# Attention and squared-ReLU MLP on one core: one copy moved, one pair of sums moved, and the last store split in two

## The chip, the cores and the metric

The kernel runs on one core of one Trainium2 chip. The metric is the device time of one execution in microseconds (us). Before the change the median of three runs is 303.92 us (303.79 to 304.94). The profiled execution took 303.61 us; its trace spans 301.6 us from the first to the last instruction, and TensorE was granted 0.998 of its full clock.

## The reference

Attention over 8 batch rows of 8 heads, 576 positions and 64 dimensions. Heads 0 to 3 look at the last 32 positions ("sliding"), heads 4 to 7 at every fourth of the last 128 ("dilated"). The result, as a matrix of 4608 tokens by 512, goes through a two-layer perceptron whose hidden layer is a ReLU squared.

```python
scores = scale * np.matmul(q, k.transpose(0, 1, 3, 2))
mask_plain = (rel >= 0) & (rel < 32)
mask_dil = (rel >= 0) & (rel < 128) & (rel % 4 == 0)
scores = np.where(masks[None], scores, -1e9)          # plain for heads 0-3, dil for 4-7
attn = softmax(scores)
x = matmul(attn, v).transpose(0, 2, 1, 3).reshape(4608, 512)
h = x @ w_in                                           # 512 -> 2048
g = np.maximum(h, 0.0) ** 2
out = g @ w_out                                        # 2048 -> 512, float32
```

## The kernel before

**Two kinds of blocks.** Attention works by batch row (576 tokens, b = 0 to 7), the perceptron by chunk (512 tokens, c = 0 to 8). The attention result x is kept transposed, in f16, in a ring `xT` of 4 rows (2304 token columns, 4 groups of 128 features). Row 7's columns start at 7 x 576 modulo 2304 = 1728; chunk 7 reads columns 1280 to 1791 and chunk 8 columns 1792 to 2303.

**The order is written out by hand.** The perceptron of a chunk is a Python generator (`moe_gen`). `pump(n)` emits its next n steps, and the attention code calls `pump` between its own pieces, so that TensorE (PE) always finds matmuls between attention's waits. Each engine then runs its own queue strictly in the order of emission, and waits at an instruction whose semaphores are not there yet.

**First layer, `mm1_gen`, lines 318 to 333.** For each of 16 hidden blocks (`ffc`), four matmuls `ph <- xT, wi` (line 302) of 512 tokens, in two steps of two. Then ScalarE (ACT) writes `rt = relu(ph)` (line 327) and VectorE (DVE) squares it into `g` (line 328). So the first layer is 32 steps. There are four PSUM buffers for `ph` and its like (`pmool`), and two for the attention results (`papool`).

**Second layer, `mm2_strassen_gen`, lines 359 to 446, for chunks 2 to 8.** It takes seven products of half-sized blocks in place of eight, in the order A, C, A, half of B, A, the other half of B, A, B. Products with sums of blocks need sums of g: `sum_of_g` (lines 335 to 338) makes `gs[0]` and `gs[1]` on DVE from four hidden blocks at a time, once after block 11 and once after block 15. Three of the weight combinations stand ready in `wt`. Every product is 16 matmuls (`pa`, `pb` or `pc`, line 381) of 256 columns, and a whole one is four steps: one for every four matmuls, the last of which also emits what closes the product. Closing is a copy by ACT from PSUM into the output tile (`take`, line 397), or an addition by DVE (`add`, line 408). The output tiles are `ou` (upper 256 tokens) and `ov` (lower 256 tokens), and `leave` (line 403) stores them from the queue of SyncE (SP). In the last chunk they leave in four stores of 256 KB, each of 256 tokens by 256 columns.

**Attention values, rows 4 to 7, `attn_values_by_dma`, lines 759 to 782.** `av_sliding` computes weighted values (`pav`, line 642) for a third of the row, and `normalize` (lines 622 to 630) divides by the row sums on DVE: a reciprocal (line 625) and a multiplication (line 630) into `xs` or `xd`. The dilated half of x is transposed by DMA into `yd`, in two pieces, and `x_from` (line 695) copies each piece into its place in `xT` on ACT. The copy of a row's second piece is put into the list `second_half` and is emitted later. For row 7 that is after `pump(20)`, that is, behind hidden block 9 of chunk 7 (lines 933 to 937). Row 7's second piece fills columns 2048 to 2303.

**Attention values, rows 1 to 3, `attn_values`, lines 728 to 757.** Here `x_sliding` (lines 667 to 680) transposes `xs` by PE (`px`, line 671) as soon as two of its three parts are there. Row 3's attention values run beside the end of chunk 2's first layer and the beginning of its second.

Of the kernel before, what the change touches and what calls it, by code (L numbers as in the profile page):

```python
# [13 lines left out]
P = 128  # L14
# [3 lines left out]
def kernel(  # L18
# [9 lines left out]
    nc = tc.nc  # L28
# [11 lines left out]
    TOKC = 512  # L40
# [40 lines left out]
    HM = DM // 2  # L81
    HF = NFF // 2
    HTOK = TOKC // 2
# [181 lines left out]
    for m, w, pad in (  # L265
# [5 lines left out]
            out=lo_[:, 0:w], in0=relf[:, 0:w], scalar1=-pad - 0.5, scalar2=None, op0=ALU.is_gt  # L271
        )
        nc.vector.tensor_scalar(
            out=hi_[:, 0:w], in0=relf[:, 0:w], scalar1=W - pad - 0.5, scalar2=None, op0=ALU.is_lt
# [6 lines left out]
    for r in range(2):  # L281
        nc.vector.tensor_scalar(
            out=vd[r][:, 0, :, :, D],
# [12 lines left out]
    def mm1_half(c, ffc, ph, dmks, parts=None):  # L296
        lo = c * TOKC % XW
        cut = min(TOKC, XW - lo)
        parts = parts or [(0, cut, lo)] + ([(cut, TOKC, 0)] if cut < TOKC else [])
        for dmk in dmks:  # L300
            for t0, t1, x0 in parts:
                nc.tensor.matmul(  # L302
                    ph[:, t0:t1],
                    wi4[ffc // 4][:, dmk, :, ffc % 4],
                    xT[:, dmk, x0 : x0 + t1 - t0],
                    start=(dmk == 0 and t0 == 0),
                    stop=(dmk == NDM - 1),
                    skip_group_check=parts != [(0, TOKC, lo)],
                )
# [3 lines left out]
    def mm1_begin(c, ffc, parts=None):  # L313
        ph = pmool.tile([P, TOKC], FP32, name=f"ph{c}_{ffc}", tag="pm")
        mm1_half(c, ffc, ph, (0, 1), parts)
        return ph

    def mm1_gen(c, g, sums=False, begun=()):
        for ffc in range(NFF):
            if ffc < len(begun):  # L320
                ph = begun[ffc]
            else:
                ph = mm1_begin(c, ffc)
                yield
            mm1_half(c, ffc, ph, (2, 3), [(T0, TOKC, T0)] if begun and ffc < len(begun) else None)
            rt = osb.tile([P, TOKC], FP16, name=f"rt{c}_{ffc}", tag="rt")
            nc.scalar.activation(rt, ph[:], ACTF.Relu)  # L327
            nc.vector.tensor_mul(g[:, ffc, :], rt, rt)  # L328
            if c == 1 and ffc % 2 == 0:
                next(w_sums)  # L330
            if sums and ffc % 4 == 3 and ffc >= HF:
                sum_of_g(g, ffc - 3, ffc + 1)
            yield

    def sum_of_g(g, f0, f1):
        k = slice(f0 - HF, f1 - HF)
        nc.vector.tensor_add(gs[0][:, k], g[:, k, HTOK:], g[:, f0:f1, HTOK:])
        nc.vector.tensor_sub(gs[1][:, k], gs[0][:, k], g[:, k, 0:HTOK])
# [20 lines left out]
    def mm2_strassen_gen(c, g):  # L359
        A, Bk, Ck = "abc"  # L360
        banks = {}

        def wq(r, q):
            return lambda k: wo[2 * r + k // 4][:, k % 4, HM * q : HM * (q + 1)]

        def gq(i, r):
            return lambda k, t: g[:, HF * r + k, HTOK * i + P * t : HTOK * i + P * (t + 1)]

        def tq(n):
            return lambda k: wt[n][:, k]  # L370

        def sq(n):
            return lambda k, t: gs[n][:, k, P * t : P * (t + 1)]

        def product(bank, a, b, ts=(0, 1)):
            new = bank not in banks
            if new:
                banks[bank] = pmool.tile([P, 2, HM], FP32, name=f"p{bank}{c}", tag="pm")
            for t in ts:
                for k in range(HF):  # L380
                    nc.tensor.matmul(  # L381
                        banks[bank][:, t],
                        a(k, t),
                        b(k),
                        start=(new and t == 0 and k == 0),
                        stop=(k == HF - 1),
                        skip_group_check=True,
                    )
                    if k % 4 == 3 and (t, k) != (ts[-1], HF - 1):
                        yield  # L390

        def half(i):
            return otp.tile([P, 2, DM], FP32, name=f"o{i}_{c}", tag="ot")

        def take(o, j):
            ot = o[:, :, HM * j : HM * (j + 1)]
            nc.scalar.copy(ot, banks[A])  # L397
            return ot

        def leave(o, i, js):  # L400
            t0 = c * TOKC + HTOK * i
            m = slice(HM * js[0], HM * (js[-1] + 1))
            nc.sync.dma_start(
                out=out[t0 : t0 + HTOK, m].rearrange("(t p) m -> p t m", p=P), in_=o[:, :, m]
            )

        def add(ot, bank):
            nc.vector.tensor_add(ot, banks[bank], ot)  # L408

        last = c == NTOKC - 1  # L410

        nc.vector.tensor_sub(g[:, 0:HF, HTOK:], g[:, 0:HF, 0:HTOK], g[:, 0:HF, HTOK:])
        yield from product(A, gq(0, 0), wq(0, 0))
        upper = half("u")
        o11 = take(upper, 0)
        yield
        yield from product(Ck, gq(0, 1), wq(1, 0))
        add(o11, Ck)
        if last:
            leave(upper, 0, (0,))  # L420
        yield
        yield from product(A, sq(1), tq(1))
        lower = half("v")
        o21 = take(lower, 0)
        nc.vector.tensor_sub(gs[1], g[:, HF:, 0:HTOK], gs[1])
        yield
        yield from product(Bk, gq(1, 0), tq(2), (0,))
        yield
        yield from product(A, sq(0), tq(0))
        o22 = take(lower, 1)  # L430
        yield
        yield from product(Bk, gq(1, 0), tq(2), (1,))
        add(o22, Bk)
        if last:
            leave(lower, 1, (1,))
        yield
        yield from product(A, sq(1), wq(1, 1))
        take(upper, 1)
        leave(upper, 0, (1,) if last else (0, 1))
        while at_end:  # L440
            at_end.pop()()
        yield
        yield from product(Bk, gq(1, 1), tq(3))
        add(o21, Bk)
        leave(lower, 1, (0,) if last else (0, 1))
        yield

    def mm2(c, g, po, t, ffc):
# [57 lines left out]
    def moe_gen(c):  # L506
        g = hidden(c)
        yield from mm1_gen(c, g, c > 1)
        yield from (mm2_strassen_gen if c > 1 else mm2_gen)(c, g)
# [10 lines left out]
    def pump(n):  # L520
        for _ in range(n):
            while pending:
                try:
                    next(pending[0])
                    break
                except StopIteration:
                    pending.pop(0)
# [317 lines left out]

    g0 = hidden(0)
    pending.append(mm1_gen(0, g0, False, begun))
    pump(1000)
    pending.append(mm2_by_rows_gen(0, g0))
# [81 lines left out]
        attn_values_by_dma(b, (copied, load_and_turn, cast, load_rest))  # L931
        pump(1000)
    pending.append(moe_gen(B - 1))
    pump(20)
    second_half.pop()()
    pending.append(moe_gen(B))
    pump(10000)
# [30 lines left out]
```

## Time and profile before

| what | before |
| --- | --- |
| time, median of 3 | 303.92 us |
| span of the trace | 301.6 us |
| PE busy | 285.4 us (95%) |
| DVE busy | 212.9 us (71%) |
| ACT busy | 172.6 us (57%) |
| POOL (GpSimd) busy | 68.1 us (23%) |
| matmuls `ph`, line 302 | 648 in 134.6 us |
| ReLU `rt`, line 327 | 144 of 609 ns |
| square `g`, line 328 | 144 of 450 ns |
| copy `xT<-yd` of a second piece, line 695 | 4 of 1098 ns |
| sums of g, lines 337 and 338 | 14 of 693 ns and 14 of 692 ns |
| last addition `ov<-pb`, line 408, and its store | 692 ns; 256 KB, 2.2 us from issue to landing |

PE is busy nearly everywhere, so the rows with much busy time are not where this change works. What counts is the few places in which PE stands idle, and the time after its last matmul. They are found in the chain of work that ended last, and in the timeline of one engine at a time.

### The profile page before, as it was taken

The page shows a single profiled execution, that of the slowest core. Times are in us where ns is not written, and L with a number is a line of the kernel's source. Part 1 is how long each engine was busy: PE and PEld are TensorE (multiplying, and loading weights), DVE is VectorE, ACT ScalarE, POOL GpSimd, SP SyncE. Part 2 cuts the span into 40 slices and gives each one's busy share as a digit, 9 for nine tenths or more (in the row PEclk, how much of TensorE's full clock was granted, in tenths as well). Part 3 has the DMA queues.
Part 4 walks back from the last instruction along what each step waited for, and adds up shares of the span by engine and source line. Part 5 has one row for each costly group of instructions (what it writes and reads, how often), then busy time and mean ns, then how long its engine had stood idle before and what let it go on. Part 6 is the DMA issues. An engine that isn't in the chain of part 4 may idle for free.

```text
span 301.6 us, 6903 instructions
## 1 busy us (share of the span) xinstructions
PE 285.4 (95%) x2768; PEld 192.6 (64%) x2768; DVE 212.9 (71%) x439; ACT 172.6 (57%) x293; POOL 68.1 (23%) x112
## 2 busy tenths in 40 slices
PE   1889999999999999999999999999999998999994
PEld 1455554555554569656989986568656964785583
DVE  7784549668843999499849985998599733824651
ACT  1956648669745952585448554845585447326620
POOL 4491009002702700530125023502140000000000
PEclk9999999999999999999999999999999999999999
DMA  7899996999599989998999799999962230003013
GB/s 117 186 203 215 205 187 111 217 192 230 136 193 181 245 153 179 224 263 125 195 175 267 152 148 171 235 236 171 171 192 42 41 139 0 3 14 127 0 36 104
DMA packets 77375, 46.60 MB, mean 155 GB/s; under 512 B 58400, under 2 KB 69152, under 8 KB 77344
## 3 DMA queue, kind: packets, MB, share of 16 engines
q1 hardware_dynamic: 68592, 32.54, 51.5%
q0 software_dynamic: 8752, 13.63, 26.3%
q8 instruction: 21, 0.34, 0.5%
q14 instruction: 10, 0.08, 0.1%
HBM read 36.70 MB, written 16.52 MB: 176 GB/s over the span
## 4 chain that ended last, share of the span: by engine, by line
PE 87%; DVE 5%; DMA 3%; ACT 2%; issue 1%; POOL 0%; POOLq 0%
PE ph L302 40%; PE pa L381 16%; PE pb L381 8%; PE po L449 7%; PE pc L381 4%; DVE AT L574 3%; PE paw L658 3%; DMA nd<-in_q_dram 3%; PE pav L642 2%; PE pz L612 2%; PE ps L587 2%; ACT AT L571 1%; PE pf L515 1%; PE py L689 1%; DVE g L328 1%
## 5 line engine op out<-in xcount | busy, mean ns | idle before, releaser
L302 PE MATMUL ph<-xT,wi 128*128 128x512 f16 (+2 forms) x648 | 134.6, 356 | 1.1 <-ACT xT L695 1.0
L327 ACT ACTIVATE rt<-ph 128x512 f16<-128x512 f32 x144 | 85.7, 609 | 45.5 <-PE ph L302 43.8
L302 PEld LDWEIGHTS <-wi 128*128 128x128 f16 x648 | 68.8, 114 | 46.0 <-issue 1.3
L328 DVE TENSOR_TENSOR g<-rt 128x512 f16<-128x512 f16 x144 | 63.0, 450 | 36.5 <-ACT rt L327 35.2
L381 PEld LDWEIGHTS <-g 128*128 128x128 f16 x448 | 43.2, 98 | 6.3 <-DVE g L328 0.2
L381 PEld LDWEIGHTS <-gs 128*128 128x128 f16 x336 | 32.5, 98 | 3.7
L449 PE MATMUL po<-wo,g 128*128 128x512 f16 x128 | 33.1, 379 | 0.0
L169 POOL CAST vp<-sv 128x512 f16<-128x512 f32 x24 | 15.5, 677 | 56.2 <-DMA sv<-in_v_dram 44.3
L381 PE MATMUL pb<-wt,g 128*128 128x256 f16 x224 | 27.9, 273 | 0.0
L408 DVE TENSOR_TENSOR ov<-pb,ov 128x512 f32<-128x512 f32 x14 | 9.7, 692 | 25.2 <-PE pb L381 19.8
L381 PE MATMUL pa<-wt,gs 128*128 128x256 f16 x224 | 27.1, 272 | 0.0
L177 POOL CAST vd<-sd 128x512 f16<-128x512 f32 (+1 forms) x32 | 22.6, 731 | 13.6 <-DMA sd<-in_v_dram 11.5
L397 ACT COPY ov<-pa 128x512 f32<-128x512 f32 x14 | 8.2, 585 | 26.8 <-PE pa L381 26.8
L630 DVE TENSOR_TENSOR xd<-paw,rcp_d 80x512 f16<-80x512 f32 (+1 forms) x32 | 21.9, 685 | 1.1
L571 ACT ACTIVATE AT<-pz 128x576 f16<-128x576 f32 x32 | 19.8, 693 | 1.2 <-PE pz L612 1.1
L574 DVE TENSOR_TENSOR AT<-AT,maskd 128x576 f16<-128x576 f16 x32 | 19.4, 634 | 1.4 <-ACT AT L571 0.9
L574 DVE TENSOR_TENSOR AT<-AT,maskp 128x576 f16<-128x576 f16 x32 | 16.9, 547 | 4.6 <-ACT AT L571 3.5
L571 ACT ACTIVATE AT<-ps 128x576 f16<-128x576 f32 x32 | 19.2, 657 | 1.4 <-PE ps L587 0.8
L397 ACT COPY ou<-pa 128x512 f32<-128x512 f32 x14 | 8.2, 585 | 19.2 <-PE pa L381 19.2
L630 DVE TENSOR_TENSOR xs<-pav,rcp_p 96x512 f16<-96x512 f32 x24 | 16.5, 687 | 0.8
L449 PEld LDWEIGHTS <-g 128*128 128x128 f16 x128 | 10.4, 98 | 8.3
L658 PEld LDWEIGHTS <-AT 128*128 128x128 f16 x256 | 12.0, 98 | 5.4 <-PE px L671 1.0
(81 smaller groups left out, 276.6 us busy)
## 6 DMA issues: line engine op xcount, KB each, us to landing
sv<-in_v_dram SPq DMA_DIRECT2D x14, 288.0 KB, 5.3
dp<-nr SPq DMA_DIRECT2D x12, 288.0 KB, 4.1
out_dram<-ou SPq DMA_DIRECT2D x6, 512.0 KB, 4.9
out_dram<-ov SPq DMA_DIRECT2D x6, 512.0 KB, 5.6
sd<-in_v_dram SPq DMA_DIRECT2D x8, 320.0 KB, 5.0
ns<-in_k_dram POOLq DMA_DIRECT2D x8, 288.0 KB, 6.6
ns<-in_q_dram POOLq DMA_DIRECT2D x8, 288.0 KB, 8.3
sd<-in_v_dram SPq DMA_DIRECT2D x8, 256.0 KB, 5.7
```

What stands on the lines that cost most here:

```text
L169: nc.gpsimd.tensor_copy(vp[b % 2][:, m : m + 2, :, 0:D], sv[:, :, m : m + 2, :].rearrange("p h m d -> p m h d"))
L177: nc.gpsimd.tensor_copy(vd[b % 2][p0:P, t, c : c + 2, :, 0:D], sd[p0:P, t, :, D * c : D * (c + 2)].rearrange("p h (c d) -> p c h d", d=D),)
L302: nc.tensor.matmul(ph[:, t0:t1], wi4[ffc // 4][:, dmk, :, ffc % 4], xT[:, dmk, x0 : x0 + t1 - t0], start=(dmk == 0 and t0 == 0), stop=(dmk ...
L327: nc.scalar.activation(rt, ph[:], ACTF.Relu)
L328: nc.vector.tensor_mul(g[:, ffc, :], rt, rt)
L381: nc.tensor.matmul(banks[bank][:, t], a(k, t), b(k), start=(new and t == 0 and k == 0), stop=(k == HF - 1), skip_group_check=True,)
L397: nc.scalar.copy(ot, banks[A])
L449: nc.tensor.matmul(po, g[:, ffc, t * P : (t + 1) * P], wo[ffc // 4][:, ffc % 4, :], start=(ffc == 0), stop=(ffc == NFF - 1),)
L571: nc.scalar.activation(AT[:, u, 0:UW], ps[:, :, 0 : UW // 2], ACTF.Exp, scale=scale)
L574: nc.vector.tensor_mul(AT[:, u, 0:UW], AT[:, u, 0:UW], mask)
L630: nc.vector.tensor_tensor(out=x, in0=pv, in1=rb, op=ALU.mult)
L658: nc.tensor.matmul(pav[:, e, h * (D + 2) : h * (D + 2) + D + 1], AT[:, 4 + h, off : off + P], vd[b % 2][:, t, 2 * a + e, h, 0 : D + 1], st ...
```

## The change

Three edits, independent of each other.

1. Row 7's second piece of x is copied into `xT` after step 44 of chunk 7 in place of step 20. 44 steps are the 32 of the first layer and the first three products (4 steps each) of the second. The copy is meant to stand on ACT where no ReLU waits behind it.
2. In chunk 2 alone, the first two sums of g are emitted after the square of hidden block 12 in place of block 11. On DVE they so come behind the normalization of row 3's first third, not ahead of it.
3. In the last chunk, the last addition and its store are split into two halves of 128 tokens. The first half is stored from SP's queue, the second from ACT's. They are meant to overlap the first half's transfer with the second half's addition.

```diff
@@ mm1_gen @@
-            if sums and ffc % 4 == 3 and ffc >= HF:
-                sum_of_g(g, ffc - 3, ffc + 1)
+            if sums and ffc == (12 if c == 2 else 11):
+                sum_of_g(g, 8, 12)
+            if sums and ffc == 15:
+                sum_of_g(g, 12, 16)
@@ mm2_strassen_gen @@
         yield from product(Bk, gq(1, 1), tq(3))
-        add(o21, Bk)
-        leave(lower, 1, (0,) if last else (0, 1))
+        if last:
+            for t, eng in enumerate((nc.sync, nc.scalar)):
+                o = o21[:, t]
+                nc.vector.tensor_add(o, banks[Bk][:, t], o)
+                t0 = c * TOKC + HTOK + P * t
+                eng.dma_start(out=out[t0 : t0 + P, 0:HM], in_=o)
+        else:
+            add(o21, Bk)
+            leave(lower, 1, (0, 1))
         yield
@@ the end @@
     pending.append(moe_gen(B - 1))
-    pump(20)
+    pump(44)
     second_half.pop()()
     pending.append(moe_gen(B))
     pump(10000)
```

## The prediction

> **What bounds the kernel now.** I read the chain of work that ended last first, because PE is busy 95% of the span and only the chain tells which idle time moves the end. Its shares are on the page:
>
> ```profile
> PE 87%; DVE 5%; DMA 3%; ACT 2%; issue 1%; POOL 0%; POOLq 0%
> ```
>
> PE's matmuls carry 87% of it, so a change pays only where the chain leaves PE. Next I read the chain in order of time. Columns: start in us, length in us, engine, tile, line. It shows this around chunk 7:
>
> ```profile
> 244.14 8.65 PE ph L302 x40
> 252.79 0.02 issue
> 252.81 0.03 ACT rt L327
> 252.84 0.47 issue
> 253.31 1.06 ACT xT L695
> 254.37 0.04 issue
> 254.41 4.69 PE ph L302 x21
> ...
> 271.33 13.81 PE ph L302 x64
> ```
>
> Chunk 8's 64 matmuls run without a break in 13.81 us. Chunk 7's are cut by an ACT copy into `xT`. PE's own timeline (the bracket is idle time and what ended it) gives the true gap:
>
> ```profile
> 249.81 3.62 PE L302 MATMUL ph<-xT,wi 128*128 128x512 f16 x16
> 254.41 1.89 PE L302 MATMUL ph<-xT,wi 128*128 128x512 f16 x8 [0.99 <-ACT xT L695]
> ```
>
> The chain's 1.62 us hole (252.79 to 254.41) is not all idle: PE ran three more matmuls in it. It stopped 0.99 us before the fourth matmul of block 10.
>
> The other idle spot is in chunk 2. PE's and then DVE's timeline:
>
> ```profile
> 109.37 0.42 PE L642 MATMUL pav<-vp,AT 128*128 128x65 f16 x8 [0.60 <-DVE xs L630]
> ```
>
> ```profile
> 106.19 0.75 DVE L328 TENSOR_TENSOR g<-rt 128x512 f16<-128x512 f16 x2
> 106.98 0.69 DVE L337 TENSOR_TENSOR gs<-g 128x1024 f16<-128x1024 f16 x1
> 107.70 0.69 DVE L338 TENSOR_TENSOR gs<-gs,g 128x1024 f16<-128x1024 f16 x1
> 108.31 0.20 DVE L625 RECIPROCAL rcp_p<-pav 96x8 f32<-96x8 f32 x1
> 108.54 0.69 DVE L630 TENSOR_TENSOR xs<-pav,rcp_p 96x512 f16<-96x512 f32 x1
> 109.15 0.75 DVE L328 TENSOR_TENSOR g<-rt 128x512 f16<-128x512 f16 x2
> 109.81 0.20 DVE L625 RECIPROCAL rcp_p<-pav 96x8 f32<-96x8 f32 x1
> 110.05 0.69 DVE L630 TENSOR_TENSOR xs<-pav,rcp_p 96x512 f16<-96x512 f32 x1
> ```
>
> The third `pav` needs the PSUM buffer that the first normalization (108.54) frees, and that stands behind two sums. DVE has no idle time in these rows.
>
> Last, the end. PE stops at 297.39; this is SP's queue:
>
> ```profile
> 298.13 0.37 SPq L403 DMA_DIRECT2D out_dram<-ov  x1
> ```
>
> With 2.2 us from issue to landing, as the page's list of DMA issues gives for 256 KB, the data are there at 300.33, and the closing semaphores run until 301.6.
>
> [...]
>
> **Edit 1, the copy.** Nothing is added or removed. In the order of instructions, the matmul of block 10 that waited for the copy loses that wait. The columns it reads (1280 to 1791) are not those that the copy writes (2048 to 2303), so the wait guarded nothing. The gain is the difference of the two undisturbed stretches: chunk 7's first layer takes 259.11 - 244.14 = 14.97 us, chunk 8's 285.15 - 271.33 = 13.82, so **1.15 us**. (The idle time of 0.99 is the lower bound; the chain's 1.62 the upper.) Does the copy wait elsewhere? It now stands on ACT between the two `take` copies of `ov`, which start at 264.38 and 267.00 and last 0.59 each. The free gap is 267.00 - 264.97 = 2.03 us and the copy needs 1.06, so 0.97 us is left over and the next `take` is on time. Behind it are only `take` copies. Chunk 8 first reads `xT` at 271.33, some 5 us after the copy. Cost: nothing, hidden in that gap.
>
> **Edit 2, chunk 2's sums.** The same DVE instructions in another order: reciprocal, `xs`, square of 12, two sums, square of 13, reciprocal, `xs`. The first `xs` then starts near 107.1 and ends near 107.8, ahead of 108.6, where PE arrives; the 0.60 us wait goes. But PE's next customer of DVE is the `px` transpose, which needs the second `xs`. In PE's timeline `px` starts at 110.93, back to back with the products before it, while the second `xs` ends at 110.05 + 0.69 = 110.74; with the 0.14 us from end to PE seen at the first one (109.23 to 109.37), `px` could start at 110.88. So it had 0.05 us of slack. In the new order the second `xs` has the same work ahead of it, since the sums still precede it. Only one 0.41 us step from square to sum (it waited for its own input) becomes about 0.35, so it ends at some 110.67 and `px` can start at 110.81. PE arrives there at 110.93 - 0.60 = 110.33 and waits. Gain 110.93 - 110.81 = **0.1 us**: the wait moves from `pav` to `px`. The sums themselves are not needed sooner: the product with `gs` begins at 114.32, four microseconds after they are ready.
>
> **Edit 3, the tail.** The one addition of 692 ns becomes two. [...]the rows of this trace give 440 (a line through 8 columns at 196 and 512 at 692). In the order of instructions the first half still waits for the end of the whole product, and the second for nothing. With T the end of PE: the first addition runs from T + 0.02 to T + 0.45; the second starts some 0.08 before that (as the square follows `xs`, 0.61 us behind a 0.69 us instruction) and ends near T + 0.80. The second store is issued at about T + 0.83, against T + 0.74 before, so 0.09 later, behind SP's first issue (T + 0.47 to T + 0.84 if it is 0.37 long again)[...]. Its transfer is half as long: before, data moved from 299.0 to 299.85, 0.85 us for 256 KB, so half saves 0.42. Landing: T + 0.83 + 2.2 - 0.42 = T + 2.61 against T + 2.94. Gain **0.3 us**. The price of a first store from ACT's queue is in no row. From below it is SP's; from above I take the slowest median landing of an output store, 5.6 us for 512 KB beside other traffic. I take SP's, because at that point nothing else moves.
>
> **Sum.** 1.15 + 0.1 + 0.3 = 1.55 us. After each edit the chain is PE alone, with no DMA in it between 11 us and the end, so all of it reaches the end: 303.92 - 1.55 = **302.37 us**, 0.51% faster. The bound of 0.5% is 302.40, so this lies on it.
>
> **The rivals.** (a) The store from ACT costs more than SP's, by some 0.3 to 1 us, and eats the tail's gain: 303.92 - 1.25 = 302.67, up to 303.4. For it: the queue is unused until then, and the second addition ends later than the single one. Against: half the data on idle DMA engines. (b) Edit 2 frees all of its 0.60 us, should the second `xs` come earlier than I order it: 303.92 - 1.15 - 0.6 - 0.3 = 301.87. Against it: DVE is full there. (c) The copy takes a new wait with it: if the next `take` is late by the whole 1.06 us, PE stands at the product behind it and edit 1 is worth 0.1: 303.92 - 0.1 - 0.4 = 303.4. Against it: 0.97 us of slack. (d) Slower than before: the first store from ACT's queue lands only after 5.6 us. Then it ends at T + 6.43 in place of T + 2.94, 3.49 later, less the 1.25 of the other edits: 306.2. For it: no row shows this queue. Against: it would have to be 3.8 us worse than SP's.
>
> **How the numbers follow.** The forecast 54%, (a) 25%, (b) 10%, (c) 6%, (d) 5%. Range: (b) and the sum with edit 1 at its upper end (302.37 - 0.47 = 301.9) set the low end at 301.8; most of (a) lies below 303.1, which leaves out (c), (d) and a little of (a). Faster by over 0.5%: all of (b) and most of the forecast's upper half and a little more, as all but one run before lie at or below 303.92, together 0.52. Slower: (d), 0.04. The rest is within.
>
> **What would show it.** Right: chunk 7's first layer takes 13.8 us from its first matmul to its second layer, and PE has no idle time put down to the `xT` copy; in chunk 2 the wait of `pav` is gone and one of some 0.5 us stands at `px` instead; the span from PE's end to the last instruction is 3.9 us, not 4.2. Wrong: an issue on ACT well over 0.4 us or a landing over 2.2 us, PE idle in chunk 7's products, or a `px` that does not wait.

## The result and the profile after

Six runs of the changed kernel have a median of 302.77 us, against 304.18 us in six runs of the kernel before. One of the changed kernel's six was slow (306.25 us), and the ratio, 0.9942 with a 95% interval of 0.9914 to 0.997, is of the fast runs alone. More runs of both in a later session gave 0.9944 (0.9925 to 0.9963). The traced execution spans 300.5 us, against 301.6.

The two traces do not start alike. Chunk 0's unbroken row of matmuls starts at 24.24 us before and at 25.10 after, and in the experiments anywhere from 23.55 to 25.55; chunk 2's first row of 18 starts at 92.94 us before and from 93.19 to 94.84 in the later traces that show it whole. What makes the difference is not shown. So I compare stretches, not absolute times.

**Chunk 7.** The chain of work that ended last, in order of time (start, length, engine, tile, line):

```profile
244.66 13.81 PE ph L302 x64
258.48 1.75 PE pa L383 x16
...
270.70 13.81 PE ph L302 x64
284.52 1.75 PE pa L383 x16
```

Chunk 7's first layer is now one stretch of 13.81 us, the same as chunk 8's; it was 14.97. ACT's timeline shows where the copy went (the bracket is idle time and what ended it):

```profile
263.75 0.58 ACT L399 COPY ov<-pa 128x512 f32<-128x512 f32 x1 [2.91 <-PE pa L383]
264.24 1.10 ACT L704 COPY xT<-yd 128x512 f16<-128x512 f16 x1
266.37 0.58 ACT L399 COPY ov<-pa 128x512 f32<-128x512 f32 x1 [1.04 <-PE pa L383]
```

It lies in what used to be idle time, and 1.04 us of that is left ahead of the next `take`.

**Chunk 2.** DVE's timeline, then PE's:

```profile
107.78 0.20 DVE L634 RECIPROCAL rcp_p<-pav 96x8 f32<-96x8 f32 x1
108.01 0.69 DVE L639 TENSOR_TENSOR xs<-pav,rcp_p 96x512 f16<-96x512 f32 x1
108.62 0.41 DVE L328 TENSOR_TENSOR g<-rt 128x512 f16<-128x512 f16 x1
108.95 0.68 DVE L339 TENSOR_TENSOR gs<-g 128x1024 f16<-128x1024 f16 x1
109.66 0.69 DVE L340 TENSOR_TENSOR gs<-gs,g 128x1024 f16<-128x1024 f16 x1
110.27 0.42 DVE L328 TENSOR_TENSOR g<-rt 128x512 f16<-128x512 f16 x1
110.61 0.20 DVE L634 RECIPROCAL rcp_p<-pav 96x8 f32<-96x8 f32 x1
110.84 0.69 DVE L639 TENSOR_TENSOR xs<-pav,rcp_p 96x512 f16<-96x512 f32 x1
```

```profile
109.47 0.42 PE L651 MATMUL pav<-vp,AT 128*128 128x65 f16 x8
109.72 0.60 PE L302 MATMUL ph<-xT,wi 128*128 128x512 f16 x2
110.16 1.04 PE L383 MATMUL pa<-wo,g 128*128 128x256 f16 x8
111.03 0.34 PE L680 MATMUL px<-ident,xs 96*128 96x96 f16 x4
111.58 0.26 PE L680 MATMUL px<-ident,xs 96*128 96x96 f16 x2 [0.22 <-DVE xs L639]
```

The third `pav` no longer waits. A wait for the second `xs` has come up at the last two of the six `px` transposes, 0.22 us by its bracket. The loss is larger. A transpose has a record of 0.21 us, yet six in a row take 0.42 us: they overlap, and idle time that is counted from the end of the last record leaves a part of the stall out. The length of the whole group holds all of it. Here are `px` and a group of product C before, then that group after and the square of block 15 on DVE that it reads, before and after:

```profile
110.93 0.42 PE L671 MATMUL px<-ident,xs 96*128 96x96 f16 x6
112.76 1.47 PE L381 MATMUL pc<-wo,g 128*128 128x256 f16 x12
```

```profile
113.25 1.67 PE L383 MATMUL pc<-wo,g 128*128 128x256 f16 x12
```

```profile
112.50 0.41 DVE L328 TENSOR_TENSOR g<-rt 128x512 f16<-128x512 f16 x1
113.29 0.41 DVE L328 TENSOR_TENSOR g<-rt 128x512 f16<-128x512 f16 x1
```

The six transposes take from 111.03 to 111.84 after, 0.81 us, so PE lost 0.39 us there. Product C lost another 0.2 us, which no bracket shows: its fourth matmul starts at 113.76, just after the square is done (113.70). Before, the square was done at 112.91 and that matmul started at 113.08 without a wait.

**The tail.** From PE's last matmul (295.00 + 1.76 = 296.76) to the end of the span it is 300.54 - 296.76 = 3.78 us; before it was 301.57 - 297.39 = 4.18. (The pages round the span to 0.1 us; for the tails I take it to 0.01 us from the trace.) DVE and the two queues, then the issues with their size and the time to landing:

```profile
296.78 0.76 DVE L449 TENSOR_TENSOR ov<-pb,ov 128x256 f32<-128x256 f32 x2 [2.75 <-PE pb L383]
297.23 0.35 SPq L451 DMA_DIRECT2D out_dram<-ov  x1
297.62 0.37 ACTq L451 DMA_DIRECT2D out_dram<-ov  x1
```

```profile
out_dram<-ov SPq DMA_DIRECT2D x1, 128.0 KB, 1.7
out_dram<-ov ACTq DMA_DIRECT2D x1, 128.0 KB, 1.7
```

The second addition ends at 297.54, later than the single one would (0.71 after PE's end, now 0.78). But a store of half the size lands 1.7 us after its issue, not 2.2.

### The profile page after: what moved, and what is told of

Same layout as the page of the kernel before. It is cut to its first block, busy times and chain, and to the rows that moved or that the text cites. A ratio compares the mean times of both kernels' runs of the same rounds, so it can differ in the third digit from the quotient of the medians.

```text
span 300.5 us, 6907 instructions
## 1 busy us (share of the span) xinstructions
PE 285.8 (95%) x2768; PEld 193.5 (64%) x2768; DVE 212.1 (71%) x440; ACT 172.7 (57%) x293; POOL 67.3 (22%) x112
## 4 chain that ended last, share of the span: by engine, by line
PE 88%; DVE 6%; DMA 2%; ACT 2%; issue 1%; POOL 0%; DVEq 0%; POOLq 0%
PE ph L302 39%; PE pa L383 16%; PE pb L383 8%; PE po L458 8%; PE pc L383 4%; DVE AT L583 3%; PE paw L667 3%; DMA ns<-in_q_dram 2%; PE ps L596 2%; PE pav L651 2%; PE pz L621 1%; PE pf L524 1%; PE pd L570 1%; DVE g L328 1%; ACT AT L580 1%; PE py L698 1%
## 5 line engine op out<-in xcount | busy, mean ns | idle before, releaser
L328 DVE TENSOR_TENSOR g<-rt 128x512 f16<-128x512 f16 x144 | 61.0, 436 | 35.8 <-ACT rt L327 34.8
L410 DVE TENSOR_TENSOR ov<-pb,ov 128x512 f32<-128x512 f32 x13 | 9.0, 691 | 22.8 <-PE pb L383 17.3
L583 DVE TENSOR_TENSOR AT<-AT,maskp 128x576 f16<-128x576 f16 x32 | 19.2, 619 | 4.6 <-ACT AT L580 3.5
L583 DVE TENSOR_TENSOR AT<-AT,maskd 128x576 f16<-128x576 f16 x32 | 18.1, 598 | 1.6 <-ACT AT L580 1.3
```

The source lines that it names most:

```text
L583: nc.vector.tensor_mul(AT[:, u, 0:UW], AT[:, u, 0:UW], mask)
```

## The experiments

### Each edit by itself

Each of these three is the kernel before with one of the three hunks of the change.

> Edit 1 alone. Theory: chunk 7's first layer takes 13.8 us in place of 14.97, PE has no idle time put down to the xT copy, and the time falls by 1.15 us against the kernel before (ratio 0.996). Rival (the copy takes its wait along): a PE wait of up to 1 us appears in chunk 7's products, between the first and the last of the seven, and the time does not move.

> Edit 2 alone. Theory from the changed kernel's trace: the 0.60 us wait of the third pav goes, a wait of 0.2 us comes at the last two of the six px transposes, and 0.37 us is won between the first square of the pair ahead of the sums and the second pa group. Time 0.3 to 0.4 us lower (ratio 0.9988). The prediction's own count: a wait of 0.5 us at px and 0.1 us won. Rival: the whole 0.60 is won.

> Edit 3 alone. Theory: from PE's last matmul to the last instruction 3.75 us in place of 4.21, so 0.45 us won (ratio 0.9985); each half lands 1.7 us after its issue. Rival: a second queue in the program costs something at the start that the tail does not show; then the first matmul of chunk 0 comes later than 22.73 us in this kernel (it was 23.60 in the changed one) and the time is the same or higher than before.

| kernel | ratio to before (95%) | chunk 2, us | chunk 7's first layer, us | PE's end to span's end, us |
| --- | --- | --- | --- | --- |
| before | 1 | 31.78 | 14.97 | 4.18 |
| copy alone | 0.9982 (0.9962 to 1.0001) | 32.01 | 13.81 | 4.17 |
| sums alone | 1.0009 (0.9992 to 1.0027) | 31.31 | 14.96 | 4.18 |
| tail alone | 1.0008 (0.9983 to 1.0032) | 31.63 | 14.96 | 3.84 |
| all three | 0.9942 (0.9914 to 0.997) | 31.61 | 13.81 | 3.78 |

"Chunk 2" is from the start of its first unbroken row of 18 matmuls to the end of its last product, both read from the chain. The stages show what the whole time cannot: a gain of 0.3 to 0.5 us (0.1 to 0.15%) is smaller than the intervals. The sums alone even came out at 1.0009, with an interval whose lower end, 0.9992, lies just above the 0.9988 that I expected; and the copy alone showed less than its 0.4%.

Whole times do not add up. The three single ratios multiply to 0.9999, and the three edits together measured 0.9942, which is further apart than their intervals explain. From chunk 2's row of 18 matmuls to the end of the span the traces of the single edits are shorter than before by 1.10, 0.59 and 0.50 us. So what is missing would have to lie ahead of that row, but one trace of each kernel does not show it, and the gap stays open. I take the traces for the mechanism, and the three together for the total.

In the sums-alone trace the list of waits shows no wait of PE for DVE between 100 and 236 us. The groups show two: the six `px` take 0.52 us and the twelve `pc` 1.66 us, 0.10 and 0.19 more than before.

The rival of the tail experiment was a cost of the second queue at the start. In its trace chunk 0's unbroken row started at 23.55 us, the earliest of all twelve traces, so it was not seen there. It isn't excluded: the seven traces with a store from ACT's queue start that row from 23.55 to 25.55 us, the five without from 24.24 to 24.91, and the time of this kernel did not fall.

### Why PE waited for the copy: two copies at the old place

```diff
 def x_from(b, t, y):
-    nc.scalar.copy(o, y.rearrange("x r c i -> x c i r"))
+    yy = y.rearrange("x r c i -> x c i r")
+    if b == B - 1 and t == 1:
+        for f in range(2):
+            nc.scalar.copy(o[:, f], yy[:, f])
+    else:
+        nc.scalar.copy(o, yy)
```

> The kernel before, with row 7's second copy left at step 20 but written as two copies, one for each of the two feature groups. A box from first to last address of one group's piece no longer covers columns that chunk 7 reads, so in the order of instructions the fourth matmul of block 10 has no wait for the copy. Theory (the cost was a wait on columns that chunk 7 does not read): chunk 7's first layer takes 13.8 us although the ReLUs of blocks 10 to 15 still stand behind about 1.1 us of copying, as four PSUM buffers of 0.86 us each take that up; 1.15 us won. Rival (ReLUs queued behind the copy starve PE): PE is idle for 0.5 to 1 us some blocks later, waiting for a ReLU, and nothing or little is won.

Ratio 0.9966 (0.9952 to 0.9981). ACT's timeline and then the chain of this kernel:

```profile
253.76 0.60 ACT L327 ACTIVATE rt<-ph 128x512 f16<-128x512 f32 x1 [0.27 <-PE ph L302]
254.25 1.17 ACT L698 COPY xT<-yd 128x256 f16<-128x256 f16 x2
255.32 1.63 ACT L327 ACTIVATE rt<-ph 128x512 f16<-128x512 f32 x3
```

```profile
245.09 13.81 PE ph L302 x64
```

The copies stand where the one copy stood, between the ReLUs of blocks 9 and 10, and take 1.17 us. Three ReLUs run one behind the other to catch up. PE is not cut. So here a copy among the ReLUs costs nothing by itself; the 1.15 us came from the matmul that waited for the copy. That the wait arose from a box from first to last address is what the edit was built on and fits what it did; the edit does not show how the boxes are reckoned.

### The second queue, or the smaller store?

The tail of the change with `(nc.sync, nc.sync)` in place of `(nc.sync, nc.scalar)`, and nothing else of the change:

> Edit 3 alone, with both halves stored from SP's queue. Theory (the gain is the smaller last transfer, not the second queue): SP's two issues of 0.36 us follow each other without a gap, the second at about the end of the second addition, and from PE's end to the end it takes 3.75 us as with two queues. Rival (the second queue is what gains): the second issue comes 0.3 us or more after the addition, or its landing takes over 2.0 us, and the tail is 4.0 us or more.

```profile
297.95 0.76 DVE L447 TENSOR_TENSOR ov<-pb,ov 128x256 f32<-128x256 f32 x2 [2.75 <-PE pb L381]
298.40 0.83 SPq L449 DMA_DIRECT2D out_dram<-ov  x2
```

SP issues both within 0.83 us. PE's end to the span's end is 301.79 - 297.93 = 3.86 us, nearly as with two queues (3.78, 3.79 and 3.84 in the three traces that have just the change's tail). So most of the gain is the smaller last store, in this one trace. The second queue brings at most 0.1 us, which these traces can't separate from nothing.

The opposite edit leaves the addition and the last store whole and moves that store to ACT's queue:

```diff
         add(o21, Bk)
-        leave(lower, 1, (0,) if last else (0, 1))
+        if last:
+            t0 = c * TOKC + HTOK
+            nc.scalar.dma_start(out=out[t0 : t0 + HTOK, 0:HM].rearrange("(t p) m -> p t m", p=P), in_=o21)
+        else:
+            leave(lower, 1, (0, 1))
```

> The kernel before, with its last store of 256 KB undivided but issued from ACT's queue. Theory (a first store from ACT costs what one from SP costs): issue 0.37 us, landing 2.2 us after it, tail 4.2 us. Rival (the unused queue is slower at first): landing over 2.5 us after the issue.

> The last store undivided from ACT's queue once more. It landed 3.3 us after its issue in the first look, against 2.2 for the same store from SP, but single stores from SP took 3 to 4 us too in some traces. Theory (a stray delay that meets either queue): landing 2.2 us, tail 4.2 us. Rival (256 KB from ACT's queue is slower): about 3.3 us again, tail 5.2 us.

The list of DMA issues of the first and of the second run:

```profile
out_dram<-ov ACTq DMA_DIRECT2D x1, 256.0 KB, 3.3
```

```profile
out_dram<-ov ACTq DMA_DIRECT2D x1, 256.0 KB, 2.9
```

The issue takes 0.42 us, but the landing was late in both, and PE's end to the span's end was 5.28 and 4.87 us. In both, one of the 16 DMA engines was still busy 0.6 to 1 us after the others had done (a DMA share of 0.06 to 0.07 in stretches of 0.2 us). The DMA queues between issue and landing tell what was different. The first run from ACT, then the same store of the kernel before, from SP:

```profile
q10 hardware_dynamic: 272, 0.26, 23.9%
q8 instruction: 1, 0.02, 2.8%
```

```profile
q1 hardware_dynamic: 272, 0.26, 35.4%
```

Queue q8 fetched 16 KB of instructions in one packet of 1.49 us, which began 0.31 us after the start of the issue (in the second run 1.09 us, also 0.31 us after it). Such a fetch stands beside late stores from SP's queue too. In seven of the twelve traces one falls among the stores after 294 us: the two here, the copy alone, the tail alone, the second trace of the changed kernel and the two kernels below that have more than the change. In each of them a store took 2.9 to 4.1 us. In the other five none took over 2.21 us. So the delay comes with the fetch and meets either queue. That the lagging engine is the one with the fetch fits but isn't shown, as the trace does not name a packet's engine. Whether a store issued by ACT calls for the fetch is open: it did not during the halves of 128 KB from ACT, which landed after 1.7 to 1.8 us in all five traces that have them.

### The changed kernel again, and with more

> The changed kernel itself, for more runs and a second trace. Theory (three gains of 1.15, some 0.4 and some 0.45 us, and a start that differs from run to run by about 1 us whatever the kernel): ratio 0.993 to 0.995; chunk 7's first layer 13.8 us; from PE's end to the end of the span 3.75 us. Rival (the earlier ratio was luck of the start, as the single edits measured 0.998, 1.001 and 1.001): ratio 0.997 or more.

Ratio 0.9944 (0.9925 to 0.9963); PE's end to the span's end 3.79 us. Its chain in chunk 2:

```profile
111.37 0.87 PE pa L383 x8
112.24 0.17 PE px L680 x4
112.44 0.26 PE px L680 x2
112.70 0.87 PE pa L383 x8
```

The chain shows a wait of only 0.03 us at `px`, but PE's timeline has the whole group:

```profile
112.08 0.62 PE L680 MATMUL px<-ident,xs 96*128 96x96 f16 x6
```

That is 0.20 us over the undisturbed 0.42. The loss is smaller than in the first trace because PE came later against DVE in this run: `px` starts 0.38 us after the second `xs` starts (111.70), there 0.19 us. The next kernel adds two edits to the change: the sums behind block 14, and the last chunk's B product in two PSUM tiles.

```diff
-            if sums and ffc == (12 if c == 2 else 11):
+            if sums and ffc == (14 if c == 2 else 11):
@@ product @@
+            apart = last and bank == Bk
             for t in ts:
+                key = (bank, t) if apart else bank      # a PSUM tile for each 128 tokens
...
@@ the end @@
             for t, eng in enumerate((nc.sync, nc.scalar)):
+                yield from product(Bk, gq(1, 1), tq(3), (t,))
                 o = o21[:, t]
-                nc.vector.tensor_add(o, banks[Bk][:, t], o)
+                nc.vector.tensor_add(o, banks[Bk, t][:, t], o)
```

The earlier addition from this product is split into two in the same way (left out here).

> The changed kernel with two more edits: chunk 2's first sums behind the square of block 14, so behind the second normalization too; and in the last chunk the B product in two PSUM tiles, one for each 128 tokens, so that the first half is added and stored while PE still makes the second. Theory: px waits for nothing, and from PE's end to the span's end it takes 3.35 us in place of 3.75, as the second addition starts at once (0.42 us) and its store is issued 0.35 us earlier; 0.4 to 0.6 us below the changed kernel (ratio to the kernel before 0.992). Rival: the third normalization comes 1.4 us later behind the sums and px's second half waits instead; then chunk 2 wins nothing.

Ratio 0.9939 (0.9917 to 0.9962), not the 0.992 expected. The tail is 301.92 - 298.50 = 3.42 us, close to the 3.35 expected. The list of waits of PE in chunk 2 shows that the first edit won nothing:

```profile
PE pc L385 <- DVE g L328: 0.2, 1, 0.2
```

`px` waits no more, but the sums now stand ahead of the square of block 15, which the product C reads. Its group of twelve loses 0.40 us (it ends at 116.40, 1.87 us after its start at 114.53), against 0.2 with the sums behind block 12, so what was won at `px` is lost there. It is not the third normalization, as the rival had it, but the effect is the rival's. So I went back to block 12 and kept only the split product:

> The changed kernel with one more edit: in the last chunk the B product in two PSUM tiles, one for each 128 tokens (chunk 2's sums stay behind block 12). Theory: 3.4 us from PE's end to the span's end, 0.35 to 0.4 us less than in the changed kernel, and at most 0.2 us of waiting in chunk 2; ratio to the kernel before 0.993. Rival: the tail's gain is lost in the second and third additions of the extra halves, or cannot be told from the changed kernel's 0.994.

```profile
296.30 0.42 DVE L455 TENSOR_TENSOR ov<-pb,ov 128x256 f32<-128x256 f32 x1 [2.12 <-PE pb L385]
296.75 0.35 SPq L457 DMA_DIRECT2D out_dram<-ov  x1
297.17 0.42 DVE L455 TENSOR_TENSOR ov<-pb,ov 128x256 f32<-128x256 f32 x1 [0.45 <-PE pb L385]
297.68 0.37 ACTq L457 DMA_DIRECT2D out_dram<-ov  x1
```

PE ends at 297.14. The first half's addition is over before that, and the tail is 300.59 - 297.14 = 3.45 us. The ratio is 0.9914 (0.9881 to 0.9948), the lowest of all. `px` and `pc` lose 0.4 us in this trace, more than the 0.2 that I allowed for. The interval of the ratio overlaps that of the changed kernel, so the 0.3 to 0.4 us are seen in the trace and not proved in the time.

## Why the prediction was right, and where not

**The total.** Forecast 302.37 us, measured 302.77; in ratios 0.9949 and 0.9942 to 0.9944. From chunk 2's row of 18 matmuls to the end of the span it is 208.63 us before and 206.75 after, and 206.91 in the second trace of the changed kernel: 1.88 and 1.72 us less, where the forecast summed to 1.55.

**Edit 1** came out to the hundredth: 14.97 to 13.82 us, the gap on ACT held the copy, and no wait came up in chunk 7's products. The 0.99 us of idle time were less than the gain because the record of a `ph` matmul is 0.38 us long, while undisturbed ones start every 0.22 us. The reading that the wait guarded nothing is borne out by the two copies at the old place.

**Edit 2** had the right mechanism and the wrong size. The wait did move from `pav` to `px`, but at `px` I forecast 0.5 us, and by the length of the group it was 0.39, 0.23, 0.20 and 0.10 us in the four traces with the sums behind block 12. The step that failed is "`px` ... needs the second `xs`": four of its six transposes read only the first `xs` and ran at once, and from the end of `xs` to PE it took 0.05 us (111.53 to 111.58), not 0.14. DVE's part was right: from the square ahead of the first normalization to the second `xs`, 106.19 to 110.05 before and 107.05 to 110.84 after, 0.07 us less. A second term was missing: PE, now earlier, loses 0.2 us in product C, waiting for the square of block 15. The two errors cancel in part.

How far DVE is behind PE also differs from run to run. The six traces without the edit that show this stretch whole take 31.51 to 32.01 us for chunk 2, mean 31.74; the four with the sums behind block 12 take 31.31 to 31.61, mean 31.45. The waits account for all of that. Counted from the start of the matmul ahead of it, `pav` loses 0.48 to 0.98 us without the edit (0.76 in the kernel before, where the bracket has 0.60). With the edit, `px` and `pc` together lose 0.29 to 0.59 us by the lengths of their groups. Chunk 2 less these losses takes 31.02 to 31.05 us in all ten traces. So the term is some 0.3 us, not 0.1, and between two single traces it can look smaller (31.78 and 31.61).

**Edit 3** was forecast at 0.3 us and is 0.34 to 0.4. Half an addition took 0.42 us; the 440 ns of the prediction was an estimate from the rows before. The second half is issued 0.86 us after PE's end and lands 1.75 us later: 2.61 us, as worked out. What two issues at once cost each other is not shown: ACT's began 0.04 us after SP's had ended, in all three traces with just this tail. From that landing to the end of the span it took 1.17 us, before 1.23. Rival (a), a dearer store from ACT, did not show with 128 KB; the whole 256 KB were late twice, both times with a fetch of instructions beside them. The first half's addition waited for the whole product, as the order of instructions said, and two PSUM tiles removed just that.

**The rivals.** (b) did not happen: `pav`'s wait went in all four traces, but `px` and product C wait in its place. Nor did (c) and (d).

## What to carry to other kernels

When PE waits for a copy, check whether it reads anything that the copy writes. If not, write the copy in pieces (here one for each feature group), or emit it elsewhere; both won the same 1.15 us here. A list of waits can hide a stall of matmuls that overlap (0.03 us in the chain at `px`, 0.20 by its length); compare the length of the same group before and after. Work moved behind one wait on a full engine brought up the next ones here (0.60 us at `pav` went, 0.39 at `px` and 0.2 in product C came), so find the next customer, and count which of its instructions really need the late operand. At the end of this kernel the size of the last store (a tail of 4.18 us undivided, 3.86 in two halves from SP) and whether its addition can start before the last product is over (3.42 and 3.45) counted for more than the queue that issues it (3.78 to 3.84 with ACT's).

## What the runs showed of the hardware

- In the five traces with no fetch of instructions among the stores after 294 us, a store of 256 KB landed 2.2 us after its issue and one of 128 KB (in two of them) 1.7 us. With a 16 KB fetch (0.9 to 1.6 us, queue q8) among them, a store took 2.9 to 4.1 us in all seven traces that have it, from SP's queue and from ACT's.
- Transposes by PE overlap: one has a record of 0.21 us, and six in a row took 0.42 us. A stall between two of them that cost 0.20 us showed as 0.03 us in the chain.
- Where the change moved work, DVE kept the order of emission: the two sums of g, emitted behind the square of block 11, started at 106.98 and 107.70 us, ahead of the first normalization (108.31); emitted behind block 12, at 108.95 and 109.66, behind it (107.78). PE stood 0.60 us at the third `pav` before, and the two `ph` matmuls behind it started after it, at 109.63.
- Two f32 additions of 256 columns back to back took 0.76 us, one of 512 columns 0.69.
- The start of chunk 0's unbroken row varied by 2 us over twelve traces (23.55 to 25.55), so edits of a few tenths are to be judged by stages of the trace.
